# q and k of batches 3 and 4 turned by transposing transfers instead of TensorE

## The chip, the cores and the metric

The kernel runs on one core of one Trainium2 chip. The metric is the device time of one execution in microseconds (us). Before the change it is 356.54 us, the median of three runs (356.33, 356.54 and 356.86).

The engines are named as the profile names them: PE is TensorE's matmul, PEld its weight load, DVE is VectorE, ACT ScalarE, POOL GpSimd and SP SyncE. A "q" behind an engine's name means its instruction queue. L358 is line 358 of the kernel.

## What is computed

Eight batches of eight heads go through causal attention with a decay bias, and the result goes through a mixer of two parts:

```python
scores = q @ k^T / sqrt(64) + min(-(cum_i - cum_j), 0)      # cum = cumsum(max(s, 0)); causal
x      = softmax(scores) @ v                                # 576 x 64 a head, heads side by side: 576 x 512
u      = x + (x^T @ U @ V)^T                                # mixing along the sequence, rank 32
out    = u + relu(u @ w_ch1) @ w_ch2                        # 512 -> 2048 -> 512, per token
```

q, k, v are float32 in HBM, (8, 8, 576, 64); the loads turn them into bf16.

## The kernel before

**Pairs and slots.** Two heads of a batch are a pair, so there are 32 pairs, n = 0 to 31, four to a batch: pairs 12 to 15 are batch 3, pairs 16 to 19 batch 4. For each pair a slot in SBUF holds q and k with the 64 features on partitions, and four more rows with parts of the cumulative sum, so that one matmul over 68 rows gives score and bias together (`scores`, L425; its matmuls are L429). In the main loop three slots take turns. `rows_of` (L300) issues from SP two small transfers that bring the four rows of a pair (L302); they may go once the slot's last scores are done.

**Two ways to turn q and k.** They come from HBM with tokens on partitions and have to be turned.

- By TensorE: for batches below `ZB` (5 before), `load_qk` loads a batch in a few large transfers from POOL (for batches 3 and 4 one each for q and k, L129, 576 KB), and `transposes` (L307) turns a pair with 16 transposes against the identity (L322, 72x128 each) into two PSUM tiles. Four copies of 64x576 out of PSUM, two for each head, put them into the slot (L342): on DVE, or on ACT for the first head of pairs 10, 14 and 18 and for some early pairs.
- By transfers: for batches from `ZB` on, `load_pairs` (L118) loads a batch by head, 16 transfers of 72 KB from POOL (L121). `turn_pair` (L356) issues from SP one transposing transfer for a pair, SBUF to SBUF, 1536 columns of 96 rows (L358), into one of three landings: one buffer of its own and the free ends of the two q/k buffers. `part_pair` (L363) then copies 64x1152 for each head from the landing into the slot, on DVE (L366).

There are two q/k buffers (`qk_sd`), used by even and odd batches. POOL's loads run over eight semaphores in turn, so a load waits until the one eight before it has landed.

**The main loop** (L1242) runs n from 8 on. In iteration n it issues loads for a later batch, `turn_pair(n + 3)`, turning or parting of pair n + 1, the scores of pair n, and `values` of pair n - 1 (L481; matmuls L493, then DVE's reciprocal L502 and scaling L503, and a transposing transfer of the result on SP, L510). Where a pair is the second of its batch, `seqmix` of the batch before goes between (L517; its additions L547 read what L510 brought). All the while single steps of `chanmix` (hidden layer L662 with ACT's RELU L1039, output layer L720 by a product scheme with seven products and sums on DVE, L698 and L734) are taken in between by `step_fill`, so that TensorE has work while softmax goes on.

**Who sets the order.** `in_program_order` pins PE and POOL to the order in which the program was written, over the whole kernel (L1314), and DVE, ACT and SP for the first part only (L1195). After that the compiling layer's scheduler orders DVE, ACT and SP by its own estimates; each engine then runs its list strictly in order and waits in place for semaphores. PSUM for `pwork` tiles is four banks; a matmul into a bank waits until the tile before it has been read.

```python
def turn_pair(n):
    b, hp = divmod(n, PB)
    nc.sync.dma_start_transpose(
        out=landing(n).rearrange("p (a m) -> p a m", m=TR),
        in_=by_pairs(b)[:, hp].rearrange("p c t two d -> p (c t two d)"),
    )
def part_pair(n):
    rows_of(n)
    for hh in range(2):
        nc.vector.tensor_copy(slot_of(n)[0:D, hh, 0 : 2 * S], landing(n)[ds(hh * D, D)])
        yield
```

Of the kernel before, what the change touches and what calls it, by code (L numbers as in the profile page):

```python
# [39 lines left out]
def kernel(  # L40
# [27 lines left out]
    KA = D + 4  # L68
    NF = FF // 128
    FT = 2  # L70
    ZB = 5
    TR, RT = 96, 6

    consts = ctx.enter_context(tc.tile_pool(name="consts", bufs=1))
# [35 lines left out]
    def by_pairs(b):  # L110
        return qk_sd[b % 2][:TR, :QK].rearrange(
            "p (hp c t two d) -> p hp c t two d", hp=PB, c=2, t=RT, two=2
        )
# [4 lines left out]
    def load_pairs(b):  # L118
        for h in range(H):
            for c, src in enumerate((q, k)):  # L120
                nc.gpsimd.dma_start(  # L121
                    out=by_pairs(b)[:, h // 2, c, :, h % 2, :],
                    in_=src[b, h].rearrange("(t p) d -> p t d", p=TR),
                )
# [54 lines left out]
    def load_v(b, parts=range(5)):  # L179
        vt = v_slot(b)  # L180
        if 0 < b < 3:
            init_v(nc.gpsimd, vt)
        for t in parts:
            rows_t = 128 if t < 4 else 64
            nc.gpsimd.dma_start(  # L185
                out=vt[:rows_t, t, :, 0:D],
                in_=v[b, :, ds(t * 128, rows_t), :].rearrange("h p d -> p h d"),
            )
# [161 lines left out]
    landings = [consts.tile([128, 2 * S], BF16, name="turned")]  # L350
    landings += [qk_sd[(ZB + i) % 2][:, ds(QK, 2 * S)] for i in range(2)]

    def landing(n):
        return landings[(n - ZB * PB) % 3]
# [7 lines that stand above are left out]
# [63 lines left out]
    def scores(n, pT, spins=()):  # L425
        slot = slot_of(n)

        def mm(dst, hh, j, lo, hi):
            nc.tensor.matmul(  # L429
                dst,  # L430
                lhsT=slot[0:KA, hh, ds(S + j * 128, 128)],
                rhs=slot[0:KA, hh, lo:hi],
                start=True,
                stop=True,
            )

        tail = None
        if spins:
            tail = pwork()
            spin(spins[0], tail)  # L440
        for hh in range(2) if n > 0 else ():
            near = pscore()
            for j in range(4):
                mm(near[:, ds(j * 128, 128)], hh, j, j * 128, j * 128 + 128)
            mm(near[:, 512:960], hh, 0, 128, S)
            mm(near[:, 960:1024], hh, 3, 512, S)
            nc.scalar.activation(pT[:, hh, 0:1024], near, EXP, scale=scale)  # L447
            if n >= PB:
                mask(pT[:, hh, 0:512].rearrange("p (a b) -> p a b", a=4), 4, 128)
            if spins:  # L450
                spin(spins[1 + hh], tail)
            yield
        mid, tail = pscore(), tail if spins else pwork()
        for hh in range(2):
            mm(mid[:, ds(hh * 512, 320)], hh, 1, 256, S)
            mm(mid[:, ds(hh * 512 + 320, 192)], hh, 2, 384, S)
            if spins and hh == 0:
                spin(spins[3], tail)
        nc.scalar.activation(  # L459
            pT[:, :, 1024:1536], mid.rearrange("p (a b) -> p a b", a=2), EXP, scale=scale  # L460
        )
        yield
        for hh in range(2):
            mm(tail[:, ds(hh * 64, 64)], hh, 4, 512, S)
        nc.scalar.activation(
            pT[:, :, 1536:1600],
            tail[:, 0:128].rearrange("p (a b) -> p a b", a=2),
            EXP,
            scale=scale,
        )  # L470
        if n >= PB:
            mask(pT[:, :, 1536:1600], 2, 64)
        yield
# [557 lines left out]
    def chanmix(g, hT=None, done=0):  # L1031
        u = uT_of.pop(g)
        if g > 0:
            hT = work.tile([128, NF, 512], BF16, tag="hT", name="hT")
            sums = {1: weight_sums, NG - 3: first_weight_sums}.get(g, lambda: iter(()))()
        for nf in range(done, NF):
            f1 = pwork()
            hidden(f1, u, nf, range(4))
            nc.scalar.activation(hT[:, nf, :], f1, RELU)  # L1039
            if g > 0:  # L1040
                next(sums, None)
            if g > 0 and nf in (12, 14):
                first_sums(hT, nf == 12)
            if g > 0 and nf == 3:
                u_sd = by_token(u)
            if nf == NF - 1:
                expanded.append(g)
            yield
        if g > 0:
            yield from outputs_by_quarters(g, hT, u_sd)  # L1050
            return
        x_sb = x_of.pop(0)
        ahead = {}
        for i in range(2):
            ahead[i] = pwork()
            for _ in outputs(ahead[i], hT, i, range(8)):
                yield
            yield
        for i in range(4):
            f2 = ahead[i] if i in ahead else pwork()  # L1060
            for _ in outputs(f2, hT, i, range(8 if i in ahead else 0, NF)):
                yield
            o_sb = work.tile([128, DM], FP32, tag="o_sb", name="o_sb", bufs=3)
            nc.vector.tensor_tensor(
                o_sb.rearrange("p (a b) -> p a b", a=4),
                f2.rearrange("p (a b) -> p a b", a=4),
                x_sb[:, :, i, :],
                op=ALU.add,
            )
            nc.sync.dma_start(out=out_flat[ds(g * 512 + i * 128, 128), :], in_=o_sb)  # L1070
            yield
# [7 lines left out]
    def step_fill():  # L1079
        pace[0] += pace[1]  # L1080
        if pace[0] < 16:
            return
        pace[0] -= 16
        if NG - 3 in expanded and not ps_tail:
            return
        while fill:
            if next(fill[0], fill) is not fill:
                return
            fill.pop(0)

    def run(gen):
        for _ in gen:
            step_fill()
# [5 lines left out]
    def fill_with(n):  # L1099
        per, pace[1] = pace[1], 16  # L1100
        for _ in range(n):
            step_fill()
        pace[1] = per


    def pT_of(n):
        if n < PB + 3:
            return pTs[n % 2] if n % PB < 2 else pT_early[n % PB - 2]
        return pTs[(n + 1) % 2]

    def step(*gens):
        for gen in gens:
            next(gen, None)
# [85 lines left out]
    def load(b):  # L1199
        alloc_qk(b)  # L1200
        for h in range(0, H, 4 if b == 2 else H):
            load_qk(b, h, 4 if b == 2 else H)
# [36 lines left out]
    weave("S8 S9 M1 S9 M1 S9 M1 M1 S9 M1 F M1")  # L1239
    fill.append(chanmix(1))  # L1240
    pace[1] = 11
    for n in range(2 * PB, NP + 2):  # L1242
        b, hp = divmod(n, PB)
        if hp == 0 and b + 1 < ZB:
            load(b + 1)
        if hp == (1 if b >= ZB else PB - 1) and ZB <= b + 2 < B:
            load_pairs(b + 2)
        if ZB * PB <= n + 3 < NP:
            turn_pair(n + 3)
        mixing = seqmix(b - 1) if hp == 1 and b > FT else iter(())  # L1250
        if b == B:
            fill_with(3)
            for _ in range(3):
                step(mixing)
                fill_with(2)
        if n > 2 * PB and n + 1 < NP:
            for at, _ in enumerate((transposes if n + 1 < ZB * PB else part_pair)(n + 1)):
                step_fill()
                if at == 0:
                    step(mixing)  # L1260
        if 2 * PB + 1 < n < NP:
            for at, _ in enumerate(scores(n, pT_of(n))):
                step_fill()
                if at == 1:
                    step(mixing)
        for _ in mixing:
            fill_with(1)
        if hp == 1 and FT < b < B:
            fill.append(chanmix(b - 1))
            pace[1] = 12 if b < 6 else 10  # L1270
        if 2 * PB < n <= NP:
            run(values(n - 1, pT_of(n - 1)))
        if hp == 0 and 2 <= b < B - 1:
            load_v(b + 1)
# [70 lines left out]
```

## Time and profile before

| | |
|---|---|
| median of three runs | 356.54 us |
| the profiled execution | 356.83 us |
| its span | 355.1 us |
| TensorE clock granted over the span | 0.999 |
| the 320 transposes on PE (L322) | from 5.3 to 155.1 us, 193 to 255 ns each as recorded |
| copies out of PSUM behind them, main loop (L342) | 34 on DVE, median 454 ns; 6 on ACT, median 635 ns |
| copies from a landing (L366) | 24 on DVE, median 455 or 456 ns |
| loads of batches 2 to 4 (L129), issue to landing | 13.8, 17.1 and 17.8 us (least, median, most) |
| loads of batches 5 to 7 (L121), issue to landing | 3.0, 5.8 and 8.4 us |
| transposing transfers of pairs (L358) | 12 issues, 114.7 to 228.3 us; SP held 1.29 to 2.46 us by each |

A recorded matmul overlaps the next one, so a row's mean is longer than the time between two starts; what a stretch costs is read from the distance of starts in the timeline. Times in the timeline are from the start of the span. The 1.7 us between the span and the execution's time lie around it. Landing times are known for POOL's loads; for SP's transfers the trace has only the single packets and the waits that they end.

### The profile page before, as it was taken

How to read it: one execution, taken by the hardware profiler on the slowest of the kernel's cores; microseconds unless marked ns; L12 is line 12 of the kernel's file. 1: busy time of each engine (PE TensorE's matmuls, PEld its weight loads, DVE VectorE, ACT ScalarE, POOL GpSimd, SP SyncE). 2: the span in 40 equal slices, each digit the busy share in tenths (PEclk: the TensorE clock that was granted, in tenths of full speed). 3: DMA queues.
4: the chain of work that ended last, by engine and by line, in shares of the span. 5: the costliest groups of instructions: out<-in, count | busy, mean ns of one | idle time of the engine just before them, and what ended most of it. 6: DMA issues, size and time to landing. Idle time of an engine off the chain costs nothing.

```text
span 355.1 us, 9319 instructions
## 1 busy us (share of the span) xinstructions
PE 345.6 (97%) x3834; PEld 250.4 (71%) x3834; DVE 266.5 (75%) x590; ACT 209.1 (59%) x316; POOL 105.5 (30%) x144
## 2 busy tenths in 40 slices
PE   8999999999999999999999999999899999999996
PEld 4685656666588657785578657876588558888885
DVE  8685776779798758995598658983878679676774
ACT  4786965847763578437743675357652555674710
POOL 8897453615046602841188013000000000000000
PEclk9999999999999999999999999999999999999999
DMA  7999999999999992999499949483022644010022
GB/s 108 156 194 201 178 183 125 140 154 134 123 66 147 167 165 31 149 169 174 93 128 158 219 89 121 66 189 39 2 65 78 112 50 101 31 61 30 31 88 92
DMA packets 161827, 40.91 MB, mean 115 GB/s; under 512 B 146424, under 2 KB 160152, under 8 KB 161784
## 3 DMA queue, kind: packets, MB, share of 16 engines
q0 software_dynamic: 104592, 18.47, 77.2%
q1 hardware_dynamic: 56904, 21.65, 34.1%
q8 instruction: 30, 0.49, 0.6%
q10 hardware_dynamic: 288, 0.20, 0.2%
q14 instruction: 13, 0.11, 0.1%
HBM read 37.25 MB, written 9.70 MB: 132 GB/s over the span
## 4 chain that ended last, share of the span: by engine, by line
PE 79%; DVE 11%; ACT 5%; issue 2%; DMA 2%; DVEq 0%; ACTq 0%
PE pwork L662 21%; PE pwork L720 12%; PE quarter L720 10%; PE pscore L429 9%; PE pwork L493 7%; PE parts L950 6%; PE pwork L681 3%; PE pwork L322 3%; DVE uT L547 3%; DMA xT<-x_sb 2%; ACT pT L447 2%; DVE slot L345 2%; DVE slot L698 2%; ACT hT L1039 2%; PE pscore L390 1%
## 5 line engine op out<-in xcount | busy, mean ns | idle before, releaser
L662 PE MATMUL pwork<-uT,w_sb 128*128 128x512 bf16 x432 | 106.9, 379 | 1.1 <-ACT hT L1039 0.9
L1039 ACT ACTIVATE hT<-pwork 128x512 bf16<-128x512 f32 x108 | 65.2, 609 | 37.6 <-PE pwork L662 37.6
L447 ACT ACTIVATE pT<-pscore 128x1024 bf16<-128x1024 f32 x56 | 56.4, 1030 | 49.4 <-PE pscore L429 48.3
L662 PEld LDWEIGHTS <-w_sb 128*128 128x128 bf16 x448 | 38.7, 98 | 37.4 <-issue 1.3
L185 POOL DMA_DIRECT2D v_slot<-in_v_dram x40 | 33.8, 859 | 79.5 <-PE pwork L493 64.8
L429 PE MATMUL pscore<-slot 68*128 68x320 bf16 (+1 forms) x500 | 55.4, 246 | 0.6 <-ACT hT L447 0.3
L429 PEld LDWEIGHTS <-slot 68*128 68x128 bf16 x564 | 41.6, 97 | 17.5 <-issue 0.9
L373 DVE TENSOR_TENSOR pT<-pT,keep 128x512 bf16<-128x512 bf16 (+1 forms) x81 | 28.6, 354 | 30.9 <-ACT pT L447 26.8
L720 PEld LDWEIGHTS <-hT 128*128 128x128 bf16 x496 | 46.4, 98 | 7.1 <-DVE uT L547 0.5
L493 PEld LDWEIGHTS <-pT 128*128 128x128 bf16 x870 | 32.6, 98 | 7.1 <-issue 1.4
L493 PE MATMUL pwork<-v_slot,pT 128*128 128x65 bf16 x870 | 35.9, 193 | 0.9 <-DVE slot L345 0.6
L503 DVE TENSOR_TENSOR x_sb<-pwork,rec 128x320 bf16<-128x320 f32 x64 | 31.2, 488 | 1.4
L459 ACT ACTIVATE pT<-pscore 128x1024 bf16<-128x1024 f32 x29 | 30.3, 1045 | 2.5 <-PE pscore L429 2.4
L720 PE MATMUL pwork<-w_sb,hT 128*128 128x256 bf16 x240 | 30.4, 272 | 0.0
L345 DVE COPY slot<-pwork 64x576 bf16<-64x576 bf16 x30 | 24.1, 803 | 6.9 <-PE pwork L322 6.4
L720 PEld LDWEIGHTS <-slot 128*128 128x128 bf16 x256 | 24.1, 98 | 4.9 <-issue 1.9
L121 POOL DMA_DIRECT2D qk_sd<-in_q_dram x24 | 17.8, 742 | 11.6 <-PE pwork L322 8.1
L720 PE MATMUL pwork<-w_sum,slot 128*128 128x256 bf16 x160 | 20.1, 272 | 1.0 <-DVE o_sb L734 1.0
L322 PEld LDWEIGHTS <-qk_sd 72*128 72x128 bf16 x320 | 14.3, 99 | 6.2 <-DMA qk_sd<-in_q_dram 0.9
L121 POOL DMA_DIRECT2D qk_sd<-in_k_dram x24 | 17.9, 744 | 2.8 <-PE pwork L720 1.0
L720 PE MATMUL quarter<-w_sb,hT 128*128 128x256 bf16 x144 | 18.0, 273 | 0.3 <-DVE uT L547 0.3
L502 DVE RECIPROCAL rec<-pwork 128x5 f32<-128x5 f32 x64 | 12.1, 190 | 8.3 <-PE pwork L493 7.9
(166 smaller groups left out, 531.5 us busy)
## 6 DMA issues: line engine op xcount, KB each, us to landing
out_dram<-o_sb SPq DMA_DIRECT2D x34, 256.0 KB
v_slot<-in_v_dram POOLq DMA_DIRECT2D x32, 128.0 KB, 7.6
w_sb<-in_moe_w_ch_dram POOLq DMA_DIRECT2D x4, 1024.0 KB, 13.0
qk_sd<-in_q_dram POOLq DMA_DIRECT2D x24, 72.0 KB, 5.9
qk_sd<-in_k_dram POOLq DMA_DIRECT2D x24, 72.0 KB, 5.8
qk_sd<-in_q_dram POOLq DMA_DIRECT2D x4, 288.0 KB, 13.6
qk_sd<-in_k_dram POOLq DMA_DIRECT2D x4, 288.0 KB, 12.5
qk_sd<-in_q_dram POOLq DMA_DIRECT2D x2, 576.0 KB, 14.4
```

The source lines that it names most:

```text
L121: nc.gpsimd.dma_start(out=by_pairs(b)[:, h // 2, c, :, h % 2, :], in_=src[b, h].rearrange("(t p) d -> p t d", p=TR),)
L185: nc.gpsimd.dma_start(out=vt[:rows_t, t, :, 0:D], in_=v[b, :, ds(t * 128, rows_t), :].rearrange("h p d -> p h d"),)
L345: copies(n, hh, par)(in_turn[:, :, :, :, par], src.rearrange("p c t m -> p c m t"))
L373: nc.vector.tensor_tensor(dst, dst, keep[:, :, 0:w].to_broadcast([128, n_tiles, w]), op=ALU.min)
L429: nc.tensor.matmul(dst, lhsT=slot[0:KA, hh, ds(S + j * 128, 128)], rhs=slot[0:KA, hh, lo:hi], start=True, stop=True,)
L447: nc.scalar.activation(pT[:, hh, 0:1024], near, EXP, scale=scale)
L459: nc.scalar.activation(pT[:, :, 1024:1536], mid.rearrange("p (a b) -> p a b", a=2), EXP, scale=scale)
L493: nc.tensor.matmul(po[:, i, :], lhsT=pT[:, hh, ds(place(j, i), 128)], rhs=vt[:, j, h, :], start=(j == 0), stop=(j == i), skip_group_check= ...
L503: nc.vector.tensor_tensor(x_sb[:, hp, :, ds(hh * D, D)], po[:, :, 0:D], rec.to_broadcast([128, 5, D]), op=ALU.mult,)
L662: nc.tensor.matmul(f1, lhsT=w1_sb[:, kt, ds(nf * 128, 128)], rhs=u[:, kt, :], start=(kt == 0), stop=(kt == 3),)
L720: nc.tensor.matmul(acc[:, i, :], lhsT=a[:, kt, ds(i * 128, 128)], rhs=b[:, kt, :], start=(begin and i == 0 and kt == 0), stop=(kt == HF - ...
L1039: nc.scalar.activation(hT[:, nf, :], f1, RELU)
```

## The change

`ZB` becomes 3, and the loads of batch 3 are issued by hand ahead of the main loop, whose own rule would begin with batch 4:

```diff
     FT = 2
-    ZB = 5
+    ZB = 3
     TR, RT = 96, 6
...
     fill.append(chanmix(1))
     pace[1] = 11
+    load_pairs(ZB)
     for n in range(2 * PB, NP + 2):
```

So pairs 12 to 19 take the second way. TensorE loses their 128 transposes, and DVE and ACT their 32 copies out of PSUM; SP gains eight transposing transfers, DVE 16 copies of 64x1152. On POOL two batches change from two loads of 576 KB each to 16 of 72 KB each. The loop's rules place the loads of batch 4 in iteration 11, those of batch 5 in iteration 13 (15 before) and those of batch 6 in iteration 17 (19 before). The first transposing transfer is issued in iteration 9 instead of 17. The landings are dealt out from pair 12 on instead of pair 20.

## The prediction, made before the changed kernel was run

> **What bounds the kernel now.** I read the page first: busy time by engine, the slices, the chain that ended last.
>
> ```profile
> PE 345.6 (97%) x3834; PEld 250.4 (71%) x3834; DVE 266.5 (75%) x590; ACT 209.1 (59%) x316; POOL 105.5 (30%) x144
> ...
> DMA  7999999999999992999499949483022644010022
> ...
> PE 79%; DVE 11%; ACT 5%; issue 2%; DMA 2%; DVEq 0%; ACTq 0%
> ```
>
> TensorE is the bound: 97% busy, 79% of the chain. What leaves PE's list is a gain, and what makes PE wait is a loss, nearly one to one. The middle line is the warning: until slice 15 (133 us) the DMA engines are full, and pairs 12 to 19, which the change turns by DMA, run from 87 to 169 us. By stretches (DMA share behind PEclk, as a mean of 16 engines; overlapping packets take it over 1):
>
> ```profile
> 80.00:90.00 10.00, 9.95 (x111) 6.08 (x108) 9.07 (x22) 7.02 (x12) 4.45 (x2) 1.00 2.04 132
> ...
> 100.00:104.00 4.00, 4.00 (x70) 3.71 (x69) 3.97 (x10) 2.52 (x6) 1.66 (x2) 1.00 0.09 16
> ```
>
> So the queues are overfull up to 100 us, then empty for four, and it is in the crowded part that the first new transfers run.
>
> **The gain on PE.** The timeline of PE shows the pitch of an iteration with and without transposes:
>
> ```profile
> 76.69 0.42 PE L322 MATMUL pwork<-identity,qk_sd 72*128 72x72 bf16 x8
> 76.95 0.62 PE L493 MATMUL pwork<-v_slot,pT 128*128 128x65 bf16 x15
> ...
> 117.35 0.61 PE L429 MATMUL pscore<-slot 68*128 68x128 bf16 x6
> ...
> 125.36 0.61 PE L429 MATMUL pscore<-slot 68*128 68x128 bf16 x6
> ...
> 162.65 0.61 PE L429 MATMUL pscore<-slot 68*128 68x128 bf16 x6
> ...
> 170.13 0.61 PE L429 MATMUL pscore<-slot 68*128 68x128 bf16 x6
> ```
>
> From scores to scores it is 8.01 us where pair 15 to 16 is turned on PE, 7.48 us where pairs come by transfers: 0.53 us. Eight transposes take 0.26 us (76.69 to 76.95), which gives the same for 16. Eight pairs: **-4.2 us**. The recorded 0.19 us of one transpose is overlap and would give six times as much; starts decide.
>
> DVE loses 28 copies of 0.454 us (12.7), gains 16 of 0.456 (7.3): 5.4 us less; ACT loses four of 0.635 (2.5). PE covers both. Where PE waits for DVE near here (0.28 us in 104 to 118, 0.7 at 150) up to 1 us may come back; I take 0. POOL needs 16 x 0.73 = 11.7 us for a batch instead of 2.25 + 2.22; the 7.2 us more lie in its waits (6.4 us before 74.6, 17.1 before 102.3). Behind them stand the value loads of batch 3, first needed at 113.3: no cost even 20 us late.
>
> **The losses: copies that wait in DVE's list.** Where the new instructions stand comes from the order of the two built programs. The scheduler puts a pair's copies where it believes the transfer done; on the chip DVE then waits in place, and everything behind it too. DVE's timeline before, at the two places:
>
> ```profile
> 74.51 0.22 DVE L373 TENSOR_TENSOR pT<-pT,keep 128x128 bf16<-128x128 bf16 x1
> 74.64 0.68 DVE L551 CAST uT<-pwork 128x64 bf16<-128x64 f32 x2
> 75.77 0.69 DVE L1064 TENSOR_TENSOR o_sb<-pwork,x_sb 128x512 f32<-128x512 f32 x1 [0.44 <-PE pwork L681]
> ...
> 92.02 0.42 DVE L373 TENSOR_TENSOR pT<-pT,keep 128x512 bf16<-128x512 bf16 x1 [0.49 <-ACT pT L447]
> 93.13 0.20 DVE L502 RECIPROCAL rec<-pwork 128x5 f32<-128x5 f32 x1 [0.69 <-PE pwork L493]
> ```
>
> *Pair 12* goes between the two L551. Its load stands behind the values of batch 2, which land at 67.5 (issued 55.2, 12.3 to landing). Then q of batch 3, eight times as much as one of the new loads, landed at 74.2: 0.84 us for each, 70.9 for the pair's four. Two output transfers that shared the engines before 70 us now stand behind the turn, worth up to 2 us: I take 69.9. The trace's packet records (1152 packets of 256 bytes for a turn, 640 for L510) have a turn done 3.2 us after its issue at 114.7, when little else ran; in a crowd turn and L510 together took 5.6 us (213.6 to 219.2) to 7.1 (179.4). I take 5: 74.9, just as DVE gets there. The two copies cost 0.9 us, and L1064 behind waits for its buffer: the output that frees it went out at 59.8, now after the turn at about 73. Values of pair 8 need L1064's bank at 76.95 and get it about 1.2 us late (0.3 to 4).
>
> *Pair 14* goes between the last two lines, so DVE reaches it at about 93. On SP its turn stands behind those of 12, 13 and 15, two small L302 groups more, four outputs, u_sd (L1026, 2048 packets) and L510 of pair 8. That is 4 x 1152 + 2048 + 640 = 7296 packets from about 71.6 on. The nearest row is that very place: u_sd, one output and one L510 ran from 78.06 to 88.02. Less 1.2 us for the output it is 8.7 us for 2688 packets, 3.25 ns each, so 23.7 us, and with four outputs (4.8) pair 14 lands at **100.1**. The far rows: 125.4 to 131.6 us (same packets, two outputs, loads thinned out) gives 1.4 ns, then SP's own order holds it to about 91, since L510 of pair 8 went out at 81.2 and pair 15's load must have landed; 179.4 to 186.4 gives 3.95 ns and 105.2. I take the nearest. SP's own holds are not small in a crowd, and a transfer that shares the engines can be what ends a chain:
>
> ```profile
> 213.73 7.28 DMA xT<-x_sb
> ```
>
> Behind pair 14's copies DVE has the reciprocal and scaling of pair 10's values, whose bank the third hidden group after them needs (97.41 before, 96.4 now by two pairs less). From landing to that bank: two copies 0.9, reciprocal 0.2, L698 0.6, mask 0.15, scaling 0.4: 2.25. PE goes on at 102.4, 5.0 us later than before. The 1.2 us of pair 12 is inside this, not added: the landing is what PE meets. From there six pairs still save 0.53 each, 3.2. Net **+1.8 us**.
>
> *L510 of pair 11* stands behind the turn of pair 18, which waits for DVE's second copy of pair 15. It was issued at 104.14 and landed at 109.2; L547 wanted it at 111.9. The turn adds 1.3 to 2.5 us on SP and 2.0 to 3.6 of packets: 0.6 to 3.4 late on the old clock, but PE is 4 us late by then. I take 0, keep 3.
>
> **A rule of the skill.** The row for pair 14 is 3.25 ns a packet, that is 3.7 us for a turn's 295 KB. The Trainium skill, "DMA: Bandwidth & Descriptors", section "Latency and other measured facts", gives transposing transfers 261 GB/s. By that a turn is an estimated 1.1 us, pair 14's landing is SP's order alone, about 91, DVE never waits, and the sum is -4.2. No turn in this trace is that fast: alone one took 2.0 us of packets (115.94 to 117.97).
>
> **Sum.** The profiled execution took 356.83 us: 356.83 + 1.8 = 358.6. It stands 0.29 above the median of 356.54, so I forecast **358.3 us**. Under 0.7 us (0.2%) either way is no change that a measurement of this kernel tells.
>
> **Rivals.**
> 1. *The turns are on time.* For: the wait table has DVE waiting for transfers hardly at all (L366 0.6 us, L547 0.2), for twelve turns in the same manner; beside loads by head, 1.4 to 1.8 ns a packet is seen. Against: all twelve ran after 114 us, with DMA half empty. Then -4.2: 352.3; with DVE's relief 351.5.
> 2. *Break-even.* Landing of pair 14 at 97.5 to 99 us: PE 2.4 to 3.9 late, 3.2 back: within 0.7.
> 3. *Worse.* 3.95 ns: landing 105.2, PE 10.1 late, 3.2 back, +6.9: 363.4. The same if L510 of pair 11 adds its 3.
> 4. *It does not do what it says.* The built program has 128 fewer matmuls on PE and eight more transposing transfers: excluded.
>
> The forecast itself is the slower side; it decides from a landing after 99 us.
>
> **Chances.** Forecast's case (landing 99 to 103, +0.7 to +4.5): 0.36. Worse than +4.5: 0.14. Break-even: 0.16. On time: 0.34. Faster 0.34, same 0.16, slower 0.50. Cases of both signs hold the chance, so the range reaches from rival 1 (352.0, some 0.06 left out below) to most of rival 3 (361.8, some 0.1 above). The forecast's own case: 357.2 to 361.0.
>
> **What would show it.** Gain: 192 transposes in L322, last before 80 us; scores from pair 15 to 16 about 7.5 us apart. Pair 12: in DVE's timeline an idle stretch ended by a DMA, or L1064 after 77. Pair 14: an idle stretch of L366 of some 7 us near 93 to 100, ended by a transposing transfer, and on PE an L662 waiting for DVE right behind the first scores of pair 12. If no L366 waits over 2 us, the step of pair 14 is wrong and rival 1 holds. Pair 11: L547 near 115 ended by xT. DMA share between 100 and 104 no longer near zero. Wrong in another way would be a wait at a place I did not name, such as rows of L302 arriving after PE wants a slot, or a loss after 170 us, where the order hardly changes.

## The result and the profile after

The changed kernel takes 367.05 us, the median of six runs (365.54 to 369.90), against 356.72 us before: a ratio of 1.0294, 95% interval 1.0265 to 1.0323. It is slower, as forecast, but by 10.3 us and not by 1.8, and outside the range. The profiled execution, at 369.90 us, is the longest of the six, so a second trace was taken (367.11 us, below); the two are read side by side.

The page of the changed kernel, the lines that answer to those of before, and under them L322 from the groups by line:

```profile
PE 345.6 (94%) x3706; PEld 248.1 (67%) x3706; DVE 260.8 (71%) x578; ACT 206.5 (56%) x312; POOL 119.7 (33%) x172
...
PE   8999999999479599999999999699999999999996
...
PEclk9999999999969899999999999999999999999999
DMA  7999999999999999899989999566002809020022
...
PE 70%; DMA 11%; DVE 10%; ACT 3%; POOL 2%; issue 2%; DVEq 0%; ACTq 0%; POOLq 0%
...
L322 PE MATMUL pwork<-identity,qk_sd 72*128 72x72 bf16 x192 | 9.8, 197 | 0.1
```

The change did what it says: 192 transposes in L322 instead of 320, 128 matmuls fewer. But PE's row, which before had not one hole, has two (slices 10 to 11 and 13) and a dent (25), and right behind the two holes the granted clock drops, which before it never did in the main loop. DMA, 2% of the chain before, is now 11% (7% in the second trace). PE's busy time is the same 345.6 us with 128 matmuls less: the rest run longer.

DVE's timeline names the first hole and the second:

```profile
91.45 0.42 DVE L373 TENSOR_TENSOR pT<-pT,keep 128x512 bf16<-128x512 bf16 x1 [0.49 <-ACT pT L447]
100.94 0.94 DVE L366 COPY slot<-qk_sd 64x1152 bf16<-64x1152 bf16 x2 [9.07 <-DMA qk_sd<-qk_sd]
101.80 0.18 DVE L502 RECIPROCAL rec<-pwork 128x5 f32<-128x5 f32 x1
...
102.76 0.48 DVE L503 TENSOR_TENSOR x_sb<-pwork,rec 128x320 bf16<-128x320 f32 x1
...
123.65 0.56 DVE L547 TENSOR_TENSOR uT<-pwork,xT 128x384 bf16<-128x384 f32 x1 [3.43 <-DMA xT<-x_sb]
```

The copies of pair 14 stop DVE for 9.07 us, with the reciprocal and scaling of pair 10's values (L502, L503) queued behind them though their data had long been there. Later, L547 of batch 2 waits 3.43 us for what L510 of pair 11 brings. PE's timeline, the same two places from PE's side:

```profile
95.55 0.61 PE L429 MATMUL pscore<-slot 68*128 68x128 bf16 x6
103.30 1.89 PE L662 MATMUL pwork<-uT,w_sb 128*128 128x512 bf16 x4 [7.15 <-DVE x_sb L503]
104.98 1.91 PE L429 MATMUL pscore<-slot 68*128 68x128 bf16 x10
...
125.07 0.98 PE L493 MATMUL pwork<-v_slot,pT 128*128 128x65 bf16 x15 [3.75 <-DVE uT L547]
...
137.54 0.61 PE L429 MATMUL pscore<-slot 68*128 68x128 bf16 x6
...
145.02 0.61 PE L429 MATMUL pscore<-slot 68*128 68x128 bf16 x6
```

Before, PE had at the first of these places:

```profile
97.41 1.03 PE L662 MATMUL pwork<-uT,w_sb 128*128 128x512 bf16 x4
```

Two things are to be seen here besides the waits. The four L662 at 103.30 take 1.89 us; the same four took 1.03 us at 97.41 before. And the gain is there too: from scores to scores (137.54 to 145.02) it is 7.48 us, where turning on PE made it 8.01. By stretches (the length, then the busy time of PE, PEld, DVE, ACT and POOL with their numbers of instructions, then PEclk, DMA share, GB/s) the clock is plain:

```profile
96.00:100.00 4.00, 0.15 (x2) 0.00 (x0) 0.00 (x0) 1.26 (x2) 3.00 (x5) 1.00 1.81 159
100.00:104.00 4.00, 0.70 (x2) 0.28 (x3) 3.00 (x9) 0.00 (x0) 0.72 (x1) 0.61 2.04 154
104.00:108.00 4.00, 4.00 (x21) 2.47 (x20) 3.96 (x8) 2.52 (x3) 0.00 (x0) 0.53 1.68 170
108.00:112.00 4.00, 4.00 (x72) 3.71 (x70) 3.49 (x11) 0.88 (x3) 1.73 (x2) 1.00 0.62 45
...
124.00:128.00 4.00, 2.93 (x31) 2.43 (x31) 2.85 (x8) 0.00 (x0) 2.67 (x4) 0.60 1.93 154
```

From 104 to 108 PE is busy throughout and gets through 21 matmuls at a granted clock of 0.53, where the next four us, at 1.00, hold 72 (of other, mostly smaller shapes). The stretch from 124 shows it again behind the second wait. Values between 0.50 and 1.00 are means over a stretch in which the clock changed; stretches that are cut where it changes have it at 0.50 and 1.00:

```profile
100.90:107.70 6.80, 4.40 (x19) 2.52 (x20) 6.66 (x16) 2.22 (x3) 0.02 (x1) 0.50 1.83 154
107.70:112.00 4.30, 4.30 (x74) 3.94 (x72) 3.79 (x11) 1.18 (x3) 1.73 (x2) 1.00 0.68 65
```

**The account.** PE runs its matmuls in the same order in both kernels, the transposes aside, so the start of each one can be set against the start of the same one before. How far the changed kernel is behind, in us:

| up to | its time before | first trace | second trace | what came in between |
|---|---|---|---|---|
| end of the first scores of pair 12 | 97.38 | -1.4 | -1.3 | transposes that are gone |
| L662 behind the wait for pair 14 | 97.41 | +5.9 | +3.9 | the wait: 7.3 and 5.2 |
| L720 | 99.6 and 100.5 | +7.9 | +6.8 | slow clock: 2.1 and 2.9 |
| L720 | 112.5 | +8.2 | +7.2 | small DVE waits less gain |
| L493 behind L547 | 113.28 | +11.8 | +11.7 | the wait: 3.6 and 4.5 |
| L720 | 115.0 | +13.3 | +13.1 | slow clock: 1.5 and 1.5 |
| a row behind the last pair turned anew | 162.8 | +10.7 | +10.6 | the gain: -2.6 both |
| to the end | 227 and on | +13.1 | +10.3 | a third wait, first trace alone: 2.4 |

Times are in us. The last line is the difference of the spans (368.2 and 365.4 against 355.1). The third wait is again an L547 (2.59 us, to 234.14) for an xT behind a turn; it is absent in the second trace, so it is not a fixed part of the change.

### The profile page after: what moved, and what is told of

Read it like the earlier page. It is cut to its first block, busy times and chain, and to the rows that moved or that the text cites. A ratio compares the mean times of both kernels' runs of the same rounds, so it can differ in the third digit from the quotient of the medians.

```text
span 368.2 us, 9118 instructions
## 1 busy us (share of the span) xinstructions
PE 345.6 (94%) x3706; PEld 248.1 (67%) x3706; DVE 260.8 (71%) x578; ACT 206.5 (56%) x312; POOL 119.7 (33%) x172
## 4 chain that ended last, share of the span: by engine, by line
PE 70%; DMA 11%; DVE 10%; ACT 3%; POOL 2%; issue 2%; DVEq 0%; ACTq 0%; POOLq 0%
PE pwork L662 21%; PE pwork L720 11%; PE quarter L720 10%; PE pscore L429 9%; PE pwork L493 7%; PE parts L950 6%; DMA xT<-x_sb 4%; DMA qk_sd<-qk_sd 2%; DMA out_dram<-o_sb 2%; PE pwork L681 2%; DMA v_slot<-in_v_dram 2%; DVE uT L547 2%; POOL qk_sd L134 1%; DVE slot L698 1%; ACT pT L447 1%
## 5 line engine op out<-in xcount | busy, mean ns | idle before, releaser
L662 PE MATMUL pwork<-uT,w_sb 128*128 128x512 bf16 x432 | 106.9, 381 | 8.1 <-DVE x_sb L503 7.2
L662 PEld LDWEIGHTS <-w_sb 128*128 128x128 bf16 x448 | 39.1, 98 | 46.0 <-DVE x_sb L503 7.9
L429 PE MATMUL pscore<-slot 68*128 68x320 bf16 (+1 forms) x500 | 56.2, 248 | 0.5 <-ACT pT L447 0.2
L720 PEld LDWEIGHTS <-hT 128*128 128x128 bf16 x496 | 47.5, 99 | 8.2 <-issue 0.8
L493 PE MATMUL pwork<-v_slot,pT 128*128 128x65 bf16 x870 | 36.7, 195 | 6.7 <-DVE uT L547 5.9
L493 PEld LDWEIGHTS <-pT 128*128 128x128 bf16 x870 | 33.3, 99 | 13.3 <-issue 7.4
L121 POOL DMA_DIRECT2D qk_sd<-in_q_dram x40 | 29.6, 740 | 15.2 <-DMA v_slot<-in_v_dram 8.3
L121 POOL DMA_DIRECT2D qk_sd<-in_k_dram x40 | 29.4, 736 | 15.5 <-DMA v_slot<-in_v_dram 6.2
L503 DVE TENSOR_TENSOR x_sb<-pwork,rec 128x320 bf16<-128x320 f32 x64 | 31.2, 488 | 1.5
L720 PE MATMUL pwork<-w_sb,hT 128*128 128x256 bf16 x240 | 31.3, 280 | 0.3 <-DVE o_sb L734 0.3
L720 PEld LDWEIGHTS <-slot 128*128 128x128 bf16 x256 | 24.1, 98 | 5.0 <-issue 1.9
L720 PE MATMUL pwork<-w_sum,slot 128*128 128x256 bf16 x160 | 20.1, 273 | 1.1 <-DVE o_sb L734 1.1
L366 DVE COPY slot<-qk_sd 64x1152 bf16<-64x1152 bf16 x26 | 12.0, 461 | 11.8 <-DMA qk_sd<-qk_sd 9.1
L720 PE MATMUL quarter<-w_sb,hT 128*128 128x256 bf16 x144 | 18.0, 273 | 0.3 <-DVE uT L547 0.3
L681 PE MATMUL pwork<-w_sb,hT 128*128 128x512 bf16 x64 | 16.3, 379 | 0.0
## 6 DMA issues: line engine op xcount, KB each, us to landing
qk_sd<-in_k_dram POOLq DMA_DIRECT2D x4, 288.0 KB, 13.3
```

What stands on the lines that cost most here:

```text
L121: nc.gpsimd.dma_start(out=by_pairs(b)[:, h // 2, c, :, h % 2, :], in_=src[b, h].rearrange("(t p) d -> p t d", p=TR),)
L429: nc.tensor.matmul(dst, lhsT=slot[0:KA, hh, ds(S + j * 128, 128)], rhs=slot[0:KA, hh, lo:hi], start=True, stop=True,)
L493: nc.tensor.matmul(po[:, i, :], lhsT=pT[:, hh, ds(place(j, i), 128)], rhs=vt[:, j, h, :], start=(j == 0), stop=(j == i), skip_group_check= ...
L503: nc.vector.tensor_tensor(x_sb[:, hp, :, ds(hh * D, D)], po[:, :, 0:D], rec.to_broadcast([128, 5, D]), op=ALU.mult,)
L662: nc.tensor.matmul(f1, lhsT=w1_sb[:, kt, ds(nf * 128, 128)], rhs=u[:, kt, :], start=(kt == 0), stop=(kt == 3),)
L720: nc.tensor.matmul(acc[:, i, :], lhsT=a[:, kt, ds(i * 128, 128)], rhs=b[:, kt, :], start=(begin and i == 0 and kt == 0), stop=(kt == HF - ...
```

## The experiments

The holds in the experiments are orders between two instructions of one engine; they add no semaphore and no work. Two helpers make them: `pinned` puts an instruction behind the one of its engine that was traced last, `behind` puts it behind one that was marked (called with `None`).

```python
def behind(tc, engine, when, issue):
    issue()
    ins = [i for i in tc.nc.cur_bb.bb.instructions if i.engine == engine][-1]
    if when is None:
        last_of[engine] = ins
    elif when and engine in last_of:
        tc.add_manual_dep(ins, last_of[engine].name, ...)
```

**1. What the transposes are worth: nothing in their place.**

```diff
-            for at, _ in enumerate((transposes if n + 1 < ZB * PB else part_pair)(n + 1)):
+            for at, _ in enumerate((transposes if n + 1 < 12 else part_pair if n + 1 >= ZB * PB else lambda m: (rows_of(m), 0))(n + 1)):
```

> The kernel before, in which pairs 12 to 19 are not turned at all: their transposes and the copies behind them are left out, only the four small rows are brought (the scores of these pairs are computed from what an earlier pair left in the slot). It measures what taking the transposes off PE is worth with nothing put in their place. By starts on PE it is 0.53 us a pair, 4.2 us: 356.72 - 4.2 = 352.5 us; with DVE's small waits gone 351.7. Rival (PE gives part of it back waiting for DVE or ACT): 354 to 356.

Measured: 351.69 us against 356.42, ratio 0.9868 (0.9851 to 0.9884). So the whole prize is 4.7 us, 0.5 more than the starts on PE gave. The prediction put DVE's relief at up to 1 us and left it out; 0.3 us of the 0.5 is seen (PE waits 0.7 us for L734 instead of 1.0), the rest is not traced. PE gives nothing back.

**2. The changed kernel again.** The same program, for a second trace.

> The changed kernel once more, for a second trace. The six times so far lie between 365.54 and 369.9, and the profiled execution was the longest. Waits that are part of the mechanism come again: L366 for pair 14 (9.07 us before), L547 of batch 2 (3.43 us). The wait of L547 near 234 us (2.59 us, 2.4 us of time) is expected to be absent or smaller: 366 to 367.5 us.

Measured: 367.11 us. L366 waits 6.96 us (9.07 in the first trace), L547 of batch 2 waits 4.33 (3.43), L547 near 234 not at all (2.59). The first two waits belong to the change; the table above has both traces.

**3. Only pair 14's copies held, first try.**

```diff
-            nc.vector.tensor_copy(slot_of(n)[0:D, hh, 0 : 2 * S], landing(n)[ds(hh * D, D)])
+            pinned(tc, E.DVE, n == 14, lambda: nc.vector.tensor_copy(slot_of(n)[0:D, hh, 0 : 2 * S], landing(n)[ds(hh * D, D)]))
```

> The changed kernel with the first and second copy of pair 14 held behind the DVE instruction that stands before them in the program's text (the scaling of pair 11's values), by an order without a semaphore; all else is as the scheduler then orders it. In the profile of the changed kernel PE stood 7.15 us behind DVE's 9.07 us wait for pair 14's transposing transfer and then ran about 1.75 us slower at a granted clock of 0.66: 8.9 us. Theory A (the place of two copies in DVE's list is the loss): 367.05 - 8.9 = 358.1 us, 356.0 to 360.0, and no L366 waits over 1 us for a DMA. Theory B (the transfers are late whatever DVE does; the wait only moves to the scores of pair 14 or to L547): 363 us or more.

Measured: 360.53 us (eight runs, 356.73 to 361.61), ratio 1.0104 (1.0074 to 1.0135): 6.5 us less than the changed kernel, just outside theory A's range. The expectation was wrong in a detail: the DVE instruction traced last was not the scaling but an L698, which the scheduler had itself moved forward, so the copy went only a little way back and still waited:

```profile
100.18 0.45 DVE L366 COPY slot<-qk_sd 64x1152 bf16<-64x1152 bf16 x1 [3.25 <-DMA qk_sd<-qk_sd]
...
118.31 0.56 DVE L547 TENSOR_TENSOR uT<-pwork,xT 128x384 bf16<-128x384 f32 x1 [1.21 <-DMA xT<-x_sb]
```

The transfer comes at about the same time (100.2 us); what changed is who stands behind its copy. PE now stands for 3.57 us at 103.6, in front of L522. That speaks for A; the hold had to be made better.

**4. Only pair 18's turn held.**

```diff
-        nc.sync.dma_start_transpose(
+        pinned(tc, E.SP, n == 18, lambda: nc.sync.dma_start_transpose(
...
-        )
+        ))
```

> The changed kernel with the turn of pair 18 held on SP behind the L510 of pair 13, where the program's text has it, instead of ahead of the L510 of pair 11. DVE's wait for pair 14 stays. In the profile of the changed kernel, L547 of batch 2 waits 3.43 us for xT, and PE 3.75 us behind it and 1.6 us more by a lower clock: 5.4 us. Theory A (the turn ahead of L510 makes it late): 367.05 - 5.4 = 361.7 us, 360.5 to 363.5. Theory B (L510 is late because of the loads that fill the engines at 114 to 130 us, not because of the turn): 366 us or more, L547 still waits about 3 us.

Measured: 366.14 us, ratio 1.0274 (1.0229 to 1.0319): nothing gained to speak of, and by the time alone theory B. The trace says otherwise. L547 of batch 2 no longer waits for xT at all, and DVE's list of waits for transfers has a new line instead:

```profile
DVE slot L366 <- DMA qk_sd<-qk_sd: 8.2, 1, 8.2
...
DVE slot L366 <- DMA turned<-qk_sd: 3.6, 1, 3.6
```

The turn went back, its copies on DVE did not, so they now wait for it (until 139.68), and PE behind them (2.26 us, from 139.30 to 141.56). One wait took the place of the other.

**5. Both of these together.** The edits of 3 and 4 in one kernel.

> Both holds of the two runs above together. Theory A, both losses independent: 367.05 - 8.9 - 5.4 = 352.8 us, 352.0 to 354.5, faster than the kernel before. If the two losses share a cause (the later one only follows from the earlier one), this equals the run with pair 14's copies held alone, within 1 us. Theory B: 360 us or more.

Measured: 366.45 us, ratio 1.0282 (1.0256 to 1.0307): 12 us above A's range. In its trace L366 waits 2.97 us for pair 14 and 6.15 us (to 138.01) for pair 18, whose copies again stood ahead of the moved turn. So a hold on one engine alone can make the place on the other worse. B's bound of 360 was met, but by a wait at a known place that A names, not by transfers that are late for everyone; the next runs tell these apart.

**6. A stop of DVE without any transfer.** The kernel before, with one long instruction, held behind the masks of pair 11 and ahead of the reciprocal of pair 10's values. `t` is a landing that no pair uses yet, filled with zeros at the start of the kernel.

```diff
+            behind(tc, E.DVE, True, lambda: nc.vector.tensor_reduce(
+                out=t[:, 0:1], in_=t[:, None, 64:1152].to_broadcast([128, 8, 1088]),
+                op=ALU.max, axis=mybir.AxisListType.XY))
```

> The kernel before, with one added DVE instruction that has nothing to do with the result (the maximum of 8704 elements of a row, an estimated 9 us) ahead of the reciprocal of pair 10's values, where DVE waits for pair 14's transfer in the changed kernel. No transfer is added. It measures what such a stop of DVE costs by itself. In the changed kernel PE lost 8.9 us there, 7.15 waiting and 1.75 by a lower clock. Theory A (a stop of DVE costs PE its length less about 2 us of cover, plus a slower clock behind it): PE waits 6 to 8 us, a granted clock of about 0.66 in the 4 us behind it, 363.5 to 366.5 us. If it stays under 361, the stop of DVE isn't what made the changed kernel slow. If L547 of batch 2 now waits for xT too, the later loss in the changed kernel follows from the earlier one.

Measured: 367.94 us, ratio 1.0321 (1.0305 to 1.0336). DVE's timeline has the added instruction:

```profile
95.02 9.21 DVE L1274 TENSOR_REDUCE turned<-turned 128x1 bf16<-128x8704 bf16 x1
```

PE's timeline has what stands behind it:

```profile
105.05 1.89 PE L662 MATMUL pwork<-uT,w_sb 128*128 128x512 bf16 x4 [8.16 <-DVE x_sb L503]
106.72 1.06 PE L429 MATMUL pscore<-slot 68*128 68x128 bf16 x6
107.60 1.58 PE L662 MATMUL pwork<-uT,w_sb 128*128 128x512 bf16 x4
```

And its stretches, with the columns as above (the granted clock and the DMA share are the two ahead of the last):

```profile
96.00:100.00 4.00, 0.46 (x10) 0.29 (x7) 4.00 (x1) 0.41 (x1) 0.00 (x0) 0.81 1.71 100
100.00:104.00 4.00, 0.00 (x0) 0.00 (x0) 4.00 (x1) 0.00 (x0) 0.00 (x0) 0.50 0.04 2
104.00:108.00 4.00, 2.95 (x11) 1.36 (x12) 3.91 (x11) 0.78 (x2) 0.00 (x0) 0.50 0.21 41
108.00:112.00 4.00, 4.00 (x42) 3.02 (x41) 3.43 (x7) 3.54 (x6) 0.00 (x0) 0.91 0.01 1
```

The stop began later than in the changed kernel (95.02), so PE waited 8.16 us and the time came out above the range; the mechanism is the one expected. PE is 8.95 us late at its first matmul behind the wait and 10.7 us a few us later: 1.8 us are the clock, with the DMA engines all but empty, so the slow clock needs no traffic. L547 waits for no xT here (PE has 0.19 us at that place). The second loss of the changed kernel is not a consequence of the first.

**7. All eight pairs' copies held, firmly.** Each copy stands behind the last scaling of values before it in the program's text; the turns are left to the scheduler.

```diff
-            nc.vector.tensor_copy(slot_of(n)[0:D, hh, 0 : 2 * S], landing(n)[ds(hh * D, D)])
+            behind(tc, E.DVE, n < 20, lambda: nc.vector.tensor_copy(slot_of(n)[0:D, hh, 0 : 2 * S], landing(n)[ds(hh * D, D)]))
...
-            nc.vector.tensor_tensor(
+            behind(tc, E.DVE, None, lambda: nc.vector.tensor_tensor(
                 x_sb[:, hp, :, ds(hh * D, D)],
```

> The changed kernel with the copies of all eight pairs 12 to 19 held on DVE behind the last scaling of values (L503) that stands before them in the program's text, so that each pair is copied about one iteration before its scores. In the earlier run only pair 14's copies were held, and what held them was an L698 that the scheduler had itself moved forward: DVE still waited 3.25 us. The turns are left to the scheduler, which now puts that of pair 18 behind the L510 of pair 11, since it needs pair 15's landing. Theory A (the transfers are in time for the scores; only their copies stood too early in DVE's list): no L366 and no L547 waits over 1.5 us for a DMA, and the time is that of the kernel without turning plus at most 2 us: 351.7 to 354 us. Theory B (too much traffic for the queues: some transfer is late for whoever waits): 358 us or more.

Measured: 353.98 us, the median of four (353.25, 353.75, 354.22 and one of 358.82, which has no trace); the ratio of the three is 0.9924 (0.9907 to 0.9940): 0.8% faster than the kernel before, and 13 us faster than the changed one, with the same transfers and the same copies. No L366 waits for a DMA. What PE still waits for in this stretch is one L547, 1.5 us:

```profile
PE pwork L493 <- DVE uT L547: 1.5, 1, 1.5
```

Theory B is out: late for whoever waits they are not, but for 1.2 us at that L547. Pair 14's copies now run at 102.38 with their transfer landed, and PE begins their scores at 116.09.

**8. The turns held as well.** As 7, with L510 marked on SP and the turns of pairs 12 to 19 behind it.

> As the run with all eight pairs' copies held, and on SP the turns of pairs 12 to 19 held behind the last L510 before them in the program's text. Theory A: the same as with the copies alone, 351.7 to 354 us, since no L510 stands behind a turn that waits. If turns issued this late miss their copies (a turn and its copies are then two iterations, about 15 us, apart), L366 waits again and it is 356 us or more. Theory B: 358 us or more.

Measured: 353.19 us, ratio 0.9897 (0.9878 to 0.9916), in theory A's range. At batch 2's L547 PE waits 0.23 us; left are 1.22 us at that of batch 3 (146.92), and one L366 waits 1.29 us for a turn.

**9. Pair 14 alone, firmly.** The hold of 7 with `n == 14`.

> The changed kernel with only pair 14's two copies moved, this time firmly: behind the scaling of pair 11's values (L503). The turns of pairs 14 and 17 share a landing, so that of pair 17 falls behind the L510 of pair 11 on SP; that of pair 18 stays ahead of it. Theory A: the wait of L366 near 92 us and the slow clock behind it go (6.0 to 8.9 us in the two traces of the changed kernel), and what is left is the wait of L547 behind the turn of pair 18, 1 to 5.4 us: 354 to 360 us, most likely 357. If 362 or more, pair 14's copies were not the first loss.

Measured: 360.90 us (359.28 to 363.65), ratio 1.0124 (1.0083 to 1.0166), 0.9 us above theory A's range. The wait for pair 14 is gone, PE is 0.5 us ahead of the kernel before at 104 us, and then the second loss comes in full, though nothing had stopped PE before:

```profile
116.83 0.56 DVE L547 TENSOR_TENSOR uT<-pwork,xT 128x384 bf16<-128x384 f32 x1 [4.83 <-DMA xT<-x_sb]
```

In this trace PE goes from level to 6.5 us behind there: 5.0 of wait and 1.5 of clock, as in the table. The profiled execution was the longest of four and has the third wait too (2.63 us of PE near 228).

**10. Pair 18 alone, its turn and its copies.** The holds of 8 with `n == 18`.

> The changed kernel with pair 18 alone moved: its turn behind the L510 of pair 13 on SP, and its copies behind the scaling of pair 15's values on DVE, so that DVE doesn't meet them before the turn (in the run with the turn alone DVE waited 3.59 us for it at 136 us, and the time hardly moved). Pair 14's wait stays. Theory A: only the wait of L547 of batch 2 and its slow clock go, 5.4 to 6.0 us: 361 to 362 us (range 359.5 to 363.5), about what the stop of DVE at pair 14 costs above the gain. If 365 or more, something else than pair 18's place stops DVE there.

Measured: 363.58 us (361.32 to 364.47), ratio 1.0200 (1.0176 to 1.0224), 0.1 us above the range's upper end. In its trace (361.32 us) L366 waits 7.15 us for pair 14, PE 5.23, PE is 7.1 us behind after the clock, and L547 of batch 2 waits for nothing.

So the two losses are separate. In medians they don't add up: the first edit alone takes 6.2 us away, the second 3.5, and run 8, which holds all eight pairs and so more than these two, 13.9. The traces have each loss in its full size wherever it stands (8.1 to 9.4 us, and 5.0 to 6.5), so the missing 4 us are in executions without a trace or belong to the other pairs' holds; no run holds just the copies of pair 14 and both ends of pair 18. The third wait is a candidate: of the seven traces of kernels with a loss left in them (the changed kernel's two and those of runs 3, 4, 5, 9 and 10) it is in two. That stays open.

**11. and 12. All pairs held, and the control.** The holds of 8 with `True` for every pair, on the changed kernel and on the one before.

> As the run with the copies and turns of pairs 12 to 19 held, now for all of pairs 12 to 31. In the kernel before, DVE waits for the turns of pairs 20 to 31 hardly at all (L366 0.6 us), so little is to be had: 352 to 353.5 us (353.19 with pairs 12 to 19 alone).

> The control: the kernel before with its twelve pairs' copies and turns held in the same way. If the holds by themselves were what made the held kernels faster, this one gains too. Theory A: within 0.7 us of the kernel before (356.5), so that the 3.3 us are the worth of the eight pairs taken from TensorE.

Measured: 351.84 us, ratio 0.9864 (0.9846 to 0.9881), 0.2 us under the range, and for the control 355.32 us, 0.9959 (0.9947 to 0.9972). The control gains 1.3 us, more than the 0.7 allowed: a little of what the holds bring is not the change's. Against the control the eight pairs are worth 3.5 us, and the held kernel beats both kernels of this study, 1.4% below the one before and 4.1% below the changed one (351.84 / 367.05).

## Why the prediction was wrong, and where it was right

**The bound and the gain: right.** -4.2 us forecast, -4.7 measured alone (run 1), and the pitch of 7.48 us is there.

**Pair 12: too dear, harmlessly.** Landing at 74.9 and 1.2 us late on PE were forecast; the transfer's last packet was through at 71.02, the copies ran at 74.59 with no wait for it, and PE lost 0.35 us between 76 and 80 us.

**Pair 14: right, with some luck.** Landing at 100.1 us forecast, copies at 100.94 and, in the second trace, 98.95. From landing to PE 2.25 us forecast, 2.36 measured in both (100.94 to 103.30, 98.95 to 101.31). PE at its first matmul behind it: 5.0 us late forecast, 5.9 and 3.9 measured. The row nearest in place, 3.25 ns a packet, held: turn 15, L510 and turn 14, 2944 packets, ran from 90.9 to the end of the wait in 3.4 ns each. That the sum met the landing is luck in part. It counted 3.7 us for turn 12, whose packets were already through, and only 4.8 us for what lies between the heaps of packets, where 8.0 us lay (71.0 to 73.8, 79.4 to 83.3 and 89.5 to 90.9); the two misses nearly cancelled. The Trainium skill's 261 GB/s ("DMA: Bandwidth & Descriptors", "Latency and other measured facts"), given there for a non-contiguous middle dimension, would have it at 1.1 us a turn, an estimate that is no use in this crowd. Where little else ran the trace of before comes near it: an L510 and a turn, 1792 packets, went through in 2.05 us (167.95 to 170.00), 1.14 ns each or 1.3 us a turn, so the 2.0 us that the prediction set against the figure was not the quickest turn.

**First failure: "PE goes on at 102.4, 5.0 us later than before. ... From there six pairs still save 0.53 each, 3.2."** It took for granted that PE goes on at full speed. It goes on at half: the granted clock stood at 0.50 from 100.9 to 107.7 us in both traces, and this cost 2.1 and 2.9 us, in run 6 without any transfer 1.8. Nothing in the trace of before could show it, since PE never stood still there for longer than 1.3 us. The Trainium skill states the rule: "TensorE: Matmul & The Clock Gate", section "Part 1: The HAM clock gate", has the clock at half after an idle window of about 3.4 us, until as long a window has been busy. By that rule a stall of 5 us has a price of some 1.7 us more, an estimate (3.4 us at half speed), and it should have been in the sum. The page's remark that the ramp is under 1% of a kernel's span is about the start of a kernel; the two in the middle of this one together cost 3.6 us in the first trace and 4.4 us in the second, 1.0 and 1.2% of the span.

The traces agree in the main and show where the size comes from. In all of them the granted clock is 1.00 or 0.50, and the instants of its changes lie whole multiples of 3.41 us apart (100.9, 107.7, 124.8 and 128.2 us in the first trace). The price is half of the time that PE works at half clock: 4.4 us in the first trace (103.30 to 107.7), 6.4 us in the second (101.31 to 107.7), so the shorter wait had the dearer clock. Of the 14 idle stretches of PE over 2 us in the traces twelve, of 2.26 to 8.16 us, were followed by half clock and cost 1.5 to 3.2 us beyond their length. The shortest of these, in run 4, lay between two of these instants, and PE was busy for only 1.04 of the 3.30 us shown first here:

```profile
139.20:142.50 3.30, 1.04 (x7) 0.47 (x7) 2.32 (x7) 0.60 (x1) 0.00 (x0) 1.00 0.18 33
142.60:145.90 3.30, 3.30 (x17) 1.72 (x15) 2.60 (x5) 2.22 (x3) 0.00 (x0) 0.50 0.90 107
```

The two without half clock, 2.16 us (changed kernel, near 234) and 2.63 us (run 9, near 228), were each split over two such windows, with PE busy for 1.95 to 2.20 us of the 3.3 to 3.4 in either. So it was not the length of the stretch alone that decided.

**Second failure: "0.6 to 3.4 late on the old clock, but PE is 4 us late by then. I take 0, keep 3."** This is the larger one: 3.6 and 4.5 us of wait and 1.5 of clock, 5.0 to 6.0 us together. Two things were wrong. The slack was 1.0 us and not 2.7: at 109.2 L510's last packet was through, but in the trace of before the steps of its semaphore, for which L547 waits, came only at 110.24 to 110.86, and L547 wanted it at 111.9. (The trace thus has landings for SP's transfers too.) With that the same working gives 2.3 to 5.1 us late on the old clock; in run 9, where PE is on time, L547 waits 4.83. And the cover did not exist. L510 of pair 11 sends what PE makes from pair 11. When PE is late, L510 is late with it: DVE's scaling of pair 11's values ended at 104.11 before and at 112.04 after, and then the turn still held SP until 113.54. A consumer that is late is no slack for a transfer whose producer is late with it. SP's list before:

```profile
104.14 1.23 SPq L510 DMA_TRANSPOSE xT<-x_sb  x1
```

And after, with the turn ahead of it:

```profile
111.54 2.00 SPq L358 DMA_TRANSPOSE turned<-qk_sd  x1
113.64 1.77 SPq L510 DMA_TRANSPOSE xT<-x_sb  x1
```

The packet records have the turn's 1152 packets from 113.73 to 117.12 us and L510's 640 behind them from 117.71 to 121.77, where they took 105.75 to 109.23 before; the semaphore was complete at 123.63. The loads of batch 5 and the values of batch 4, issued from 110 on, run in the same stretch, so a packet is slow there; but with the turn out of the way (runs 4 and 10) L547 of batch 2 doesn't wait.

**The range.** It left out the worse half of rival 3, in which both losses meet. Its 363.4 plus "the same if L510 of pair 11 adds its 3" is 366.4, close to what came, but by chance: the landing was not at 105.2, and the clock is not in it. I treated as two alternatives what the profile lets happen one after the other, and gave that side 0.14.

## What to carry to other kernels

A transfer that replaces work on the bounding engine is paid where its consumer stands in an in-order list: look at what is queued behind that consumer, because the same copies with the same transfers gave 367 or 352 us by their places in the lists, and hold both ends (the transfer and what waits for it), since holding one moves the wait. Count a transfer as landed when its semaphore is, not with its last packet. Never count the lateness of a consumer as slack for a transfer whose producer is late by the same cause. And price a stall of a busy TensorE above its length: here 1.5 to 3.2 us more for each idle stretch of 3.28 us and over, and for one of 2.26.

## What the runs showed of the hardware

An idle PE is enough to set off the slow clock (run 6: DMA share 0.04 and 0.21 at a granted 0.50). A transposing transfer's semaphore was complete 1.6 us after its last packet in the kernel before (L510 of pair 11), and in the first trace after 0.9 us (pair 14's turn, at 100.82) and 1.9 us (L510 of pair 11). In the crowd SP's queue and POOL's got packets through one for one: 1653 and 1654 from 84 to 88 us in the first trace of the changed kernel, 0.42 and 0.21 MB. Times of the kernels in which transfers are late vary more: 365.54 to 369.90 us for the changed kernel, 361.32 to 364.47 in run 10 and one execution of 358.82 among four near 354 in run 7, against 355.24 to 355.33 for the control. What the longest of them waited for has a trace only in the first case, the L547 near 234 us.
